# Scoring one attention unit ahead of the mix before it, and fetching value weights on GpSimd's queue

## The chip, the cores and the metric

One core of a Trainium2 chip runs the whole kernel in one launch. The metric is the device time of that launch in microseconds (us); the figure for a kernel is the median over its runs. The engines are called PE (TensorE, the matmuls), DVE (VectorE), ACT (ScalarE), POOL (GpSimd) and SP (SyncE, which here only issues transfers).

## The reference

The inputs are float32: 2048 tokens of width 512, 32 heads of 16 channels, and a feed-forward block with 1792 hidden channels. Each token attends to eight tokens: itself and those 2, 4, ... 14 positions before it.

```python
idx = pos[:, None] - (jnp.arange(8) * 2)[None, :]
logits = jnp.einsum("bhsd,bhswd->bhsw", q, k[:, :, idx]) * Dh ** -0.5
logits = jnp.where(idx >= 0, logits, -1e9)
a = jnp.einsum("bhsw,bhswd->bhsd", softmax(logits), v[:, :, idx]) @ wo
b = (gelu(x @ w_gate) * (x @ w_up)) @ w_down
g = sigmoid((x * gate_w).sum(-1, keepdims=True))
return g * a + (1 - g) * b
```

## The kernel before, in words

**Two parities.** Since the attention step is 2, even and odd tokens never meet. The kernel treats them as two parities, 0 and 1, of 1024 tokens each, and goes through keys and values of parity 0, its feed-forward block `ffn(0)`, then keys (`keys(1)`), values (`values(1)`) and `ffn(1)` of parity 1. At the end `out_first` and `finish` multiply the attention output of parity 0 and of parity 1 with `wo`. All products keep float32 accuracy by splitting each operand into a high and a low part and doing three matmuls.

**The feed-forward block** runs over 14 blocks of 128 hidden channels. For each, seven gate and up products of parts of the weights go to PSUM (L749), ACT copies them out with `copy` and `add` (L754, L760), DVE adds them (L761, L765), ACT takes the Gelu (L866) and the factor (L850), and DVE and ACT split the product into `hh` and `hl`. For each pair of blocks, `down` multiplies them with `w_down` (L798) into four accumulators `acc` and four banks `p` whose sums ACT saves and reloads (L792, L813).

**The attention runs on DVE beside that.** A parity has four units of 128 channels (8 heads), written (0,0) to (1,3). A unit is done in three steps:

- `scores` (L536, L539): four multiplies of the queries with eight shifted keys in tile `kq`, each followed by a sum over the head's 16 channels, into the tile `lg`; `lg` has two buffers, `kq` one.
- `softmax`: max (L550), subtract (L552), Exp on ACT (L554), sum (L555), reciprocal (L557), for parity 1 the gate (L559), multiply (L561). One tile `m` of one buffer holds max and sum.
- `mix`: loads the values into the tile `v` (one buffer) with two transfers (L520, L521), then four times a multiply (L575) and three adds (L579, L581, L583); after each two of these a transpose (L588) into `tb`, and four stores `os<-tb` on SP (L590).

`channels` reads a stored half unit back (`raw<-os`, L1008), splits it (L87 on ACT, L88 on DVE) and so gives `out_first` and `finish` their operands (matmuls at L1030). `load_o` splits `wo` (L231, L132 on ACT) and lets transfers on POOL's queue form the low parts (L232).

**What sets the order.** `attention()` is a generator; after each DVE step it yields an estimate of that step's time. The feed-forward code calls `pull(budget)` at fixed places, which emits as many attention steps as the budget pays for, at a lower priority. A scheduler then decides the order of the instructions on each engine from priorities, its own model of the times, and the buffers of the pools. After that, each engine works through its list strictly in that order. Before the change, `attention()` handles unit after unit: softmax of unit i, `load_kq` of unit i+1 if its keys are there, mix of unit i, scores of unit i+1.

**Value weights.** `values` of parity 1 needs 14 parts of weights of 258 KB each that were stored to device memory earlier; `fetch_v` (L207, L209) reads them back during `keys(1)` and the start of `values(1)`, into the tiles `c`, `g0` and `g1`.

Of the kernel before, what the change touches and what calls it, by code (L numbers as in the profile page):

```python
# [10 lines left out]
F32 = mybir.dt.float32  # L11
# [5 lines left out]
P = 128  # L17
# [3 lines left out]
NP = NT // 2  # L21
# [6 lines left out]
UC = 128  # L28
UH = UC // DH
# [2 lines left out]
BEHIND = 150  # L32
PACE = (1.05, 1.22)
LOAD = 4.0
BT = 4
MASKED = -1e9 * DH ** 0.5
LOWS = (4, 8, 10), (4, 6, 8, 10, 12)
# [8 lines left out]
def tile_gated_mix(ctx: ExitStack, tc: tile.TileContext, xt, wqkv, wff, wo, out):  # L46
    nc = tc.nc
    ctx.enter_context(nc.allow_non_contiguous_dma(reason="rows of 512 bytes"))
    pool = ctx.enter_context(tc.tile_pool(name="sb", bufs=1))
# [15 lines left out]
    def bank(tag):  # L65
        return psum.tile([P, 512], F32, name=tag, bufs=BUFS.get(tag, 1))
# [30 lines left out]
    for par in range(2):  # L97
# [4 lines left out]
        for u in range(NU):  # L102
            for half in range(2):
                OS[par, u, half] = dram.tile([4, 32, 4, BT * 32], F32, name=f"os{par}{u}{half}")

# [34 lines left out]
    VW, VR, VO, SLOT = 2 * WQ, {}, {}, []  # L140
# [17 lines left out]
    def load_v(*names):  # L158

        if not PLACES:  # L160
            t = pool.tile([P, 2 * NP - 1, UC], F32, name="v").rearrange("p a c -> p (a c)")
            u = pool.tile([P, 2, BT * UC], F32, name="tb").rearrange("p a c -> p (a c)")
            PLACES.extend([t[:, i * VW:(i + 1) * VW] for i in range(3)] + [u[:, :VW]])
# [35 lines left out]
    VS_W, keep_v = {}, []  # L199
# [6 lines left out]

    def fetch_v(n):  # L207
        for i in range(2):
            nc.sync.dma_start(VO[n][i].bitcast(F32), VS_W[n][i])  # L209

# [136 lines left out]
    def values(par, bg, step, ks=range(7)):  # L349
# [14 lines left out]
        def stage():  # L364
            return tl(next(stages))[:, :512]

        def copy(o, i):
            nc.scalar.activation(o, i, AF.Copy)

        def store(st, jj, hh):  # L370
            nc.sync.dma_start(rows(VS[par, hh][:, W:], jj), st.rearrange("p (c d) -> p c d", c=2))

        for k, (a, b) in enumerate((("a11", "b11"), ("a12", "b21"), ("s1", "t1"), ("s4", "b22"), ("s2", "t2"),
                                    ("s3", "t3"), ("a22", "t4"))):
            if k not in ks:
                continue
            for t in range(BT):
                if k == 0:
# [24 lines left out]
                elif k == 5:  # L403
                    copy(US[t][:, :CU], ps[:, :CU])
                    nc.vector.tensor_tensor(PS[t], PS[t], US[t], op=OP.add)
                    store(PS[t][:, CU:], t, 1)
                    store(PS[t][:, :CU], BT + t, 1)
                else:
                    if k == 1 or not par:
                        ST[t] = stage()  # L410
                    jj, st = (t, ST[t][:, :CU]) if k == 1 else (BT + t, ST[t][:, CU:])
                    copy(st, ps[:, :CU])
# [16 lines left out]
    def keys(prep, bg):  # L429
# [4 lines left out]
        for k, (a, b) in enumerate(KEYS[:5]):  # L434
# [3 lines left out]
            if k == 0:  # L438
                C.update((t, bank(f"acc{t}")) for t in range(BT))
                for t in range(BT):  # L440
# [62 lines left out]
    LG = {}  # L503

    def load_kq(par, u):
        hh, c = divmod(u, 2)
        kq = KQ.pop() if KQ else pool.tile([P, 3 * NP - 1, UC], F32, name="kq")
        k, q = kq[:, :2 * NP - 1], kq[:, 2 * NP - 1:]
        LG[par, u] = k, q
        if not (par or u):  # L510

            nc.gpsimd.memset(k[:1, :NP - 1], 0.0)
            for a, b in (1, P - 15), (P - 15, P):
                nc.sync.dma_start(k[a:b, :NP - 1], k[a - 1:b - 1, NP:])
            return
        load_slots(k, KS[par, hh][c], paced)
        paced(nc.sync.dma_start(q, QS[par, hh][c].rearrange("(p j) d -> p j d", j=NP)))

    def load_slots(t, src, hold=lambda x: x):
        hold(nc.sync.dma_start(t[:, :NP - 1], src[:S // 2].rearrange("(p j) d -> p j d", j=NP)[:, 1:]))  # L520
        hold(nc.sync.dma_start(t[:, NP - 1:], src[W:].rearrange("(p j) d -> p j d", j=NP)))  # L521

    def spans(t, jj):

        a = t[:, jj:jj + W, :]
        return bass.AP(a.tensor, a.offset, [a.ap[0], [UC, 2], [UC, W], [1, UC]])

    def two_of(lg, jj):
        return lg[:, :, jj:jj + 2].rearrange("p h j w -> p (j w) h")

    def scores(par, u):
        k, q = LG[par, u]
        lg = pool.tile([P, UH, NP, W], F32, name="lg", bufs=2)
        for jj in range(0, NP, 2):
            prod = pool.tile([P, 2, W, UC], F32, name="prod")
            paced(nc.vector.tensor_tensor(prod, spans(k, jj), q[:, jj:jj + 2, None, :].to_broadcast([P, 2, W, UC]),  # L536
                                          op=OP.mult))
            yield 2.3
            nc.vector.tensor_reduce(two_of(lg, jj), prod.rearrange("p j w (h d) -> p (j w) h d", d=DH), axis=AX.X,  # L539
                                    op=OP.add)  # L540
            yield 2.3
        first = lg[:1, :, :NP - 1, :W - 1]
        nc.vector.tensor_tensor(first, first, mask[:1, None, :NP - 1, :W - 1].to_broadcast([1, UH, NP - 1, W - 1]),
                                op=OP.min)
        LG[par, u] = lg

    def softmax(par, u):
        lg = LG[par, u]
        m = pool.tile([P, UH, NP], F32, name="m")
        nc.vector.tensor_reduce(m, lg, axis=AX.X, op=OP.max)  # L550
        yield 0.7
        nc.vector.tensor_tensor(lg, lg, m[:, :, :, None].to_broadcast([P, UH, NP, W]), op=OP.subtract)  # L552
        yield 0.7
        nc.scalar.activation(lg, lg, AF.Exp, scale=DH ** -0.5)  # L554
        nc.vector.tensor_reduce(m, lg, axis=AX.X, op=OP.add)  # L555
        yield 0.7
        nc.vector.reciprocal(m, m)  # L557
        if par:
            nc.vector.tensor_tensor(m, m, g[:, par, None, :].to_broadcast([P, UH, NP]), op=OP.mult)  # L559
        yield 0.4  # L560
        nc.vector.tensor_tensor(lg, lg, m[:, :, :, None].to_broadcast([P, UH, NP, W]), op=OP.mult)  # L561
        yield 0.7

    def mix(par, u, pause):
        lg = LG.pop((par, u))
        hh, c = divmod(u, 2)
        v = pool.tile([P, 2 * NP - 1, UC], F32, name="v")
        load_slots(v, VS[par, hh][c])
        yield pause
        tb = pool.tile([P, 2, BT * UC], F32, name="tb")  # L570
        for jj in range(0, NP, 2):
            if jj % BT == 0:
                o = pool.tile([P, 4, BT, 32], F32, name="o")
            prod = pool.tile([P, 2, W, UC], F32, name="prod")
            paced(nc.vector.tensor_tensor(prod.rearrange("p j w (h d) -> p (j w) h d", d=DH),  # L575
                                          spans(v, jj).rearrange("p j w (h d) -> p j w h d", d=DH),
                                          two_of(lg, jj)[:, :, :, None].to_broadcast([P, 2 * W, UH, DH]), op=OP.mult))
            yield 2.3
            nc.vector.tensor_tensor(prod[:, :, :4], prod[:, :, :4], prod[:, :, 4:], op=OP.add)  # L579
            yield 1.2  # L580
            nc.vector.tensor_tensor(prod[:, :, :2], prod[:, :, :2], prod[:, :, 2:4], op=OP.add)  # L581
            two = [prod[:, :, i].rearrange("p j (b c) -> p b j c", b=4) for i in range(2)]
            nc.vector.tensor_tensor(o[:, :, jj % BT:jj % BT + 2], *two, op=OP.add)  # L583
            yield 1.1

            if jj % BT == BT - 2:
                t = tb[:, jj // BT]
                nc.vector.transpose(t, o.rearrange("p b t c -> p (b t c)"))  # L588
                for a in range(4):
                    nc.sync.dma_start(OS[par, u, jj // BT][:, :, a].rearrange("b i c -> i b c"),  # L590
                                      t[32 * a:32 * a + 32].rearrange("p (b c) -> p b c", b=4))
                yield 0.7

    done = set()
# [13 lines left out]
    def need(*key):  # L608
        while key not in done:
            yield None  # L610

    def attention():
        units = [(0, u) for u in range(NU)] + [(1, u) for u in range(NU)]
        yield from need(0, 0)
        yield from scores(0, 0)
        yield from need(0, 1)
        scored, mixed = 1, False
        for i, un in enumerate(units):
            if scored == i:
                yield from need(un[0], un[1] // 2 * 2)  # L620
                load_kq(*un)
                yield LOAD
                yield from scores(*un)
                scored += 1
                mixed = False
            yield from need(un[0], 1)
            yield from softmax(*un)


            to = units[scored] if scored < len(units) else None  # L630
            ahead = i and to and (to[0], to[1] // 2 * 2) in done
            if ahead:
                load_kq(*to)
            yield from mix(*un, LOAD if mixed else 0.0)
            done.add((*un, "o"))
            mixed = not ahead
            if ahead:
                yield from scores(*to)
                scored += 1

    fill = attention()
    credit, FILL, AFTER = [0.0], [], []

# [447 lines left out]
    for kc in range(KC):  # L1091
        name, i = ("b11", "b21")[kc // 2], kc % 2
# [222 lines left out]
```

## Time and profile before

| what | value |
|---|---|
| median of 3 runs | 611.03 us (609.93 to 612.69) |
| profiled execution, own time | 608.94 us |
| its span | 607.2 us |
| mean granted TensorE clock | 0.991 |
| PE busy | 589.2 us, 97% of the span |
| DVE busy | 535.0 us, 88% |
| ACT busy | 426.6 us, 70% |
| POOL busy | 122.8 us, 20% |
| DMA | 142.76 MB, mean 235 GB/s |

The profile shows one execution. Its rows name a line of the kernel, the engine, the operation, and output and input tiles. A timeline row has the start, the busy time, and in brackets the idle time before it on that engine and who ended it. A waits row has the sum, the number and the longest of the waits of one kind. "PEld" is the loading of weights into TensorE, which overlaps the matmuls. "SPq" or "POOLq" is the queue in which an engine issues transfers; the time shown is that of the issue, and "us to landing" is from there until the data is in place.

### The profile page before, as it was taken

What the parts mean: (1) busy time and instruction counts of PE and PEld (TensorE: products, weight loads), DVE (VectorE), ACT (ScalarE), POOL (GpSimd) and SP (SyncE); (2) the same over time, 40 slices, a digit from 0 to 9 for tenths busy, and PEclk for the clock granted to TensorE, in tenths of its full rate; (3) what the DMA queues carried; (4) which work ended last, traced back from release to release, by engine and by line L of the source; (5) the groups of instructions that cost most, each with busy time, mean ns of one, the idle gap of its engine ahead of it and who ended that gap; (6) DMA issues with size and microseconds to landing.
All of it is one profiled execution on the core that took longest, in us unless ns stands there. A gap on an engine that the chain in (4) does not pass through costs nothing.

```text
span 607.2 us, 8273 instructions
## 1 busy us (share of the span) xinstructions
PE 589.2 (97%) x2743; PEld 490.5 (81%) x2743; DVE 535.0 (88%) x623; ACT 426.6 (70%) x755; POOL 122.8 (20%) x143
## 2 busy tenths in 40 slices
PE   9999999999999999999999999999999999989983
PEld 7889888888888888888888878888878888868872
DVE  6989988999899987999978998999699979979790
ACT  6778677677888778868658646777787687945611
POOL 0230840121012120112003831121212121303100
PEclk9999999999999999999999999999999999999996
DMA  8789999898978988999898999688978998887424
GB/s 308 228 234 287 314 302 257 244 259 218 271 211 251 244 243 189 278 306 322 241 340 249 253 256 290 165 237 212 252 196 221 238 247 224 208 212 138 53 62 146
DMA packets 89320, 142.76 MB, mean 235 GB/s; under 512 B 8639, under 2 KB 49983, under 8 KB 89278
## 3 DMA queue, kind: packets, MB, share of 16 engines
q1 hardware_dynamic: 67470, 106.91, 54.1%
q0 software_dynamic: 21520, 34.94, 32.2%
q8 instruction: 21, 0.34, 0.2%
q10 hardware_dynamic: 288, 0.39, 0.2%
q14 instruction: 21, 0.17, 0.1%
HBM read 69.83 MB, written 46.49 MB: 192 GB/s over the span
## 4 chain that ended last, share of the span: by engine, by line
PE 85%; DMA 7%; ACT 3%; issue 2%; POOL 2%; SPq 0%; DVE 0%; POOLq 0%; ACTq 0%
PE p L749 39%; PE acc L798 12%; PE p L798 12%; PE acc L475 9%; PE p L1030 5%; PE p L361 3%; DMA qs<-rt 2%; PE acc L361 2%; PE p L475 2%; PE acc L1030 2%; DMA S<-raw 1%; DMA raw<-os 1%; POOL qs L483 1%; DMA g<-ws 1%; DMA g<-vwt 1%
## 5 line engine op out<-in xcount | busy, mean ns | idle before, releaser
L749 PE MATMUL p<-S,g 128*128 128x512 f32 x672 | 167.7, 389 | 0.0
L749 PEld LDWEIGHTS p<-S,g 128*128 128x128 f32 x672 | 125.8, 188 | 25.7
L749 PE MATMUL p<-A,g 128*128 128x512 f32 x504 | 126.1, 390 | 0.2 <-ACT c L760 0.2
L749 PEld LDWEIGHTS p<-A,g 128*128 128x128 f32 x504 | 94.3, 188 | 20.3 <-ACT c L760 0.7
L575 DVE TENSOR_TENSOR prod<-v,lg 128x2048 f32<-128x2048 f32 x32 | 72.9, 2278 | 0.6
L539 DVE TENSOR_REDUCE lg<-prod 128x128 f32<-128x2048 f32 x32 | 73.0, 2281 | 0.2
L536 DVE TENSOR_TENSOR prod<-kq 128x2048 f32<-128x2048 f32 x32 | 72.9, 2277 | 0.1
L798 PE MATMUL p<-d,hh 128*128 128x512 f32 x224 | 68.2, 390 | 0.2 <-ACT p L792 0.2
L708 POOL DMA_DIRECT2D g<-raw x26 | 22.5, 866 | 211.3 <-ACT g L705 101.8
L798 PE MATMUL acc<-d,hh 128*128 128x512 f32 x224 | 59.4, 389 | 0.0
L760 ACT ACTIVATE c<-p 128x512 f32<-128x512 f32 x56 | 33.5, 597 | 35.1 <-PE p L749 35.0
L798 PEld LDWEIGHTS p<-d,hh 128*128 128x128 f32 x224 | 42.0, 188 | 9.3 <-ACT p L792 0.7
L798 PEld LDWEIGHTS acc<-d,hh 128*128 128x128 f32 x224 | 42.1, 188 | 8.7
L761 DVE TENSOR_TENSOR c<-c,s 128x512 f32<-128x512 f32 x56 | 37.9, 684 | 5.6 <-ACT c L760 5.4
L798 PE MATMUL p<-d,hl 128*128 128x512 f32 x112 | 42.0, 390 | 0.0
L765 DVE TENSOR_TENSOR c<-c 128x512 f32<-128x512 f32 x56 | 38.3, 684 | 2.1 <-ACT c L866 2.0
L579 DVE TENSOR_TENSOR prod<-prod 128x1024 f32<-128x1024 f32 x32 | 39.0, 1220 | 0.1
L754 ACT ACTIVATE s<-p 128x512 f32<-128x512 f32 x56 | 33.1, 593 | 7.0 <-PE p L749 6.8
L475 PE MATMUL acc<-d,S 128*128 128x512 f32 x144 | 35.2, 391 | 0.1
L798 PE MATMUL acc<-d,hl 128*128 128x512 f32 x112 | 35.1, 389 | 0.0
L813 ACT ACTIVATE rt<-p 128x512 f32<-128x512 f32 x48 | 28.0, 595 | 9.6 <-PE p L798 9.3
L740 POOL DMA_DIRECT2D d<-r x23 | 20.1, 873 | 68.9 <-ACT d L739 54.4
(219 smaller groups left out, 1064.4 us busy)
## 6 DMA issues: line engine op xcount, KB each, us to landing
g<-raw POOLq DMA_DIRECT2D x26, 512.0 KB, 6.9
ws<-g SPq DMA_DIRECT2D x14, 768.0 KB, 6.0
g<-ws SPq DMA_DIRECT2D x14, 768.0 KB, 7.7
r<-wff SPq DMA_DIRECT2D x28, 256.0 KB, 4.4
raw<-wff SPq DMA_DIRECT2D x14, 512.0 KB, 4.7
d<-r POOLq DMA_DIRECT2D x23, 256.0 KB, 7.2
ws<-raw SPq DMA_DIRECT2D x14, 384.0 KB, 5.3
raw<-ws SPq DMA_DIRECT2D x14, 384.0 KB, 4.4
```

Source lines behind the costliest of these rows:

```text
L475: LAST[:] = [nc.tensor.matmul(ps, x[:, ts], w, start=(start and kc == i == 0), stop=(kc == 1 and i == 2), skip_group_check=True)]
L536: paced(nc.vector.tensor_tensor(prod, spans(k, jj), q[:, jj:jj + 2, None, :].to_broadcast([P, 2, W, UC]), op=OP.mult))
L539: nc.vector.tensor_reduce(two_of(lg, jj), prod.rearrange("p j w (h d) -> p (j w) h d", d=DH), axis=AX.X, op=OP.add)
L575: paced(nc.vector.tensor_tensor(prod.rearrange("p j w (h d) -> p (j w) h d", d=DH), spans(v, jj).rearrange("p j w (h d) -> p j w h d", d=D ...
L579: nc.vector.tensor_tensor(prod[:, :, :4], prod[:, :, :4], prod[:, :, 4:], op=OP.add)
L749: LAST[:] = [nc.tensor.matmul(ps, w_, a_, start=(start and kc == 0 and n == 0), stop=(kc == 1 and n == 2), skip_group_check=True)]
L754: nc.scalar.activation(s, ps, AF.Copy)
L760: nc.scalar.activation(c, ps, AF.Copy)
L761: nc.vector.tensor_tensor(c, c, s, op=OP.add)
L765: nc.vector.tensor_tensor(ge, ge, up, op=OP.mult)
L798: LAST[:] = [nc.tensor.matmul(pp, a[:, ts], w, start=(i == 0 and n == 0 and gr == 0), stop=(i == 1 and n == 2), skip_group_check=True)]
L1030: LAST[:] = [nc.tensor.matmul(pa, a, b, start=(first and n == 0), stop=(last and n == 2), skip_group_check=True)]
```

## The change

The softmax is cut in two: `exps` (max, subtract, Exp) and `shares` (sum, reciprocal, gate, multiply). The loading of `v` is taken out of `mix` into `load_values`. From unit 1 on (`PIPE = 1`, counted over all eight units), if the keys of the next unit are there, `attention()` emits: values of unit i, scores of unit i+1, keys of unit i+2, max, subtract and Exp of unit i+1, then the mix of unit i, then sum, reciprocal and multiply of unit i+1. Unit (0,0) keeps the old order. `fetch_v` issues on GpSimd's queue instead of SyncE's. No arithmetic changes. Lines further down move by about 32 numbers: L749 becomes L781, L798 L830, L1030 L1062, L575 L585, L554 L557, L1008 L1040.

```diff
@@ -32,6 +32,9 @@
 BEHIND = 150
 PACE = (1.05, 1.22)
 LOAD = 4.0
+
+
+PIPE = 1
 BT = 4
 MASKED = -1e9 * DH ** 0.5
 LOWS = (4, 8, 10), (4, 6, 8, 10, 12)
@@ -206,7 +209,7 @@
 
     def fetch_v(n):
         for i in range(2):
-            nc.sync.dma_start(VO[n][i].bitcast(F32), VS_W[n][i])
+            nc.gpsimd.dma_start(VO[n][i].bitcast(F32), VS_W[n][i])
 
 
 
@@ -544,7 +547,7 @@
                                 op=OP.min)
         LG[par, u] = lg
 
-    def softmax(par, u):
+    def exps(par, u):
         lg = LG[par, u]
         m = pool.tile([P, UH, NP], F32, name="m")
         nc.vector.tensor_reduce(m, lg, axis=AX.X, op=OP.max)
@@ -552,6 +555,10 @@
         nc.vector.tensor_tensor(lg, lg, m[:, :, :, None].to_broadcast([P, UH, NP, W]), op=OP.subtract)
         yield 0.7
         nc.scalar.activation(lg, lg, AF.Exp, scale=DH ** -0.5)
+
+    def shares(par, u):
+        lg = LG[par, u]
+        m = pool.tile([P, UH, NP], F32, name="m")
         nc.vector.tensor_reduce(m, lg, axis=AX.X, op=OP.add)
         yield 0.7
         nc.vector.reciprocal(m, m)
@@ -561,12 +568,15 @@
         nc.vector.tensor_tensor(lg, lg, m[:, :, :, None].to_broadcast([P, UH, NP, W]), op=OP.mult)
         yield 0.7
 
-    def mix(par, u, pause):
-        lg = LG.pop((par, u))
+    VT = {}
+
+    def load_values(par, u):
         hh, c = divmod(u, 2)
-        v = pool.tile([P, 2 * NP - 1, UC], F32, name="v")
+        VT[par, u] = v = pool.tile([P, 2 * NP - 1, UC], F32, name="v")
         load_slots(v, VS[par, hh][c])
-        yield pause
+
+    def mix(par, u):
+        lg, v = LG.pop((par, u)), VT.pop((par, u))
         tb = pool.tile([P, 2, BT * UC], F32, name="tb")
         for jj in range(0, NP, 2):
             if jj % BT == 0:
@@ -611,32 +621,54 @@
 
     def attention():
         units = [(0, u) for u in range(NU)] + [(1, u) for u in range(NU)]
+        scored, ready, shared = [0], [], []
+
+        def keyed(i):
+            return i < len(units) and (units[i][0], units[i][1] // 2 * 2) in done
+
+        def logits(i):
+            if units[i] not in LG:
+                load_kq(*units[i])
+                yield LOAD
+            yield from scores(*units[i])
+            scored.append(i)
+
         yield from need(0, 0)
         yield from scores(0, 0)
         yield from need(0, 1)
-        scored, mixed = 1, False
+        mixed = False
         for i, un in enumerate(units):
-            if scored == i:
+            if i not in scored:
                 yield from need(un[0], un[1] // 2 * 2)
-                load_kq(*un)
+                yield from logits(i)
+                mixed = False
+            if i not in ready:
+                if i >= PIPE and keyed(i + 1):
+                    load_kq(*units[i + 1])
+                yield from exps(*un)
+            yield from need(un[0], 1)
+            if i not in shared:
+                yield from shares(*un)
+            pipe, ahead = i >= PIPE and keyed(i + 1), i and keyed(i + 1)
+            if not pipe and ahead:
+                load_kq(*units[i + 1])
+            load_values(*un)
+            if pipe:
+                yield from logits(i + 1)
+                if keyed(i + 2):
+                    load_kq(*units[i + 2])
+                yield from exps(*units[i + 1])
+                ready.append(i + 1)
+            elif mixed:
                 yield LOAD
-                yield from scores(*un)
-                scored += 1
-                mixed = False
-            yield from need(un[0], 1)
-            yield from softmax(*un)
-
-
-            to = units[scored] if scored < len(units) else None
-            ahead = i and to and (to[0], to[1] // 2 * 2) in done
-            if ahead:
-                load_kq(*to)
-            yield from mix(*un, LOAD if mixed else 0.0)
+            yield from mix(*un)
             done.add((*un, "o"))
             mixed = not ahead
-            if ahead:
-                yield from scores(*to)
-                scored += 1
+            if pipe:
+                yield from shares(*units[i + 1])
+                shared.append(i + 1)
+            elif ahead:
+                yield from logits(i + 1)
 
     fill = attention()
     credit, FILL, AFTER = [0.0], [], []
```

Where the instructions stand now is shown at three places near the end, all around unit (1,3), the last one.

**VectorE, from the last scores of unit (1,3).** `kq`, `lg_5041` (before) and `lg_4856` (after) belong to unit (1,3), `v_4853` and `lg_4337` to unit (1,2). Before:

```order
L539 TENSOR_REDUCE lg_5041<-prod_5192 128x16x8
L543 TENSOR_TENSOR lg_5041<-lg_5041,mask_102 1x8x7x7
L550 TENSOR_REDUCE m_5251<-lg_5041 128x64
L552 TENSOR_TENSOR lg_5041<-lg_5041,m_5251 128x512
L555 TENSOR_REDUCE m_5251<-lg_5041 128x64
L557 RECIPROCAL m_5251<-m_5251 128x64
L559 TENSOR_TENSOR m_5251<-m_5251,g_136 128x64
L88 TENSOR_TENSOR hl_5601<-raw_5526,hh_5600 128x4x4x32
L561 TENSOR_TENSOR lg_5041<-lg_5041,m_5251 128x512
L575 TENSOR_TENSOR prod_5299<-v_5294,lg_5041 128x2048
```

After:

```order
L585 TENSOR_TENSOR prod_5066<-v_4853,lg_4337 128x2048
L553 TENSOR_REDUCE m_5054<-lg_4856 128x64
L589 TENSOR_TENSOR prod_5066<-prod_5066 128x2x512
L555 TENSOR_TENSOR lg_4856<-lg_4856,m_5054 128x512
L591 TENSOR_TENSOR prod_5066<-prod_5066 128x2x256
L793 TENSOR_TENSOR c_5129<-c_5129,s_5099 128x512
L593 TENSOR_TENSOR o_5065<-prod_5066 128x4x64
L797 TENSOR_TENSOR c_5119<-c_5119,c_5129 128x512
L585 TENSOR_TENSOR prod_5121<-v_4853,lg_4337 128x2048
L562 TENSOR_REDUCE m_5297<-lg_4856 128x64
L793 TENSOR_TENSOR c_5148<-c_5148,s_5075 128x512
L589 TENSOR_TENSOR prod_5121<-prod_5121 128x2x512
```

Before, sum stands directly behind subtract, with Exp on another engine between them, and the mix follows. Now the mix of unit (1,2) stands there: its first multiply ahead of the max, its adds between max, subtract and sum.

**ScalarE, the Exp of unit (1,3).** Before, it stands late, among the copies of `out_first` (L1047) and the scalings of the accumulators (L802):

```order
L1047 ACTIVATE s_5500<-p_5487,g_136 128x512
L792 ACTIVATE p_5576<-rt_3962 128x512
L554 ACT_TABLE_LOAD
L554 ACTIVATE lg_5041<-lg_5041 128x512
L1047 ACTIVATE r_5516<-p_5503,g_136 128x512
L802 ACTIVATE acc0_3735<-acc0_3735,gc_137 128x512
```

After, it stands in the last feed-forward blocks:

```order
L742 ACTIVATE g1_5101<-raw_4917 128x1024
L845 ACTIVATE rt_3825<-p_5133 128x512
L557 ACT_TABLE_LOAD
L557 ACTIVATE lg_4856<-lg_4856 128x512
L792 ACTIVATE c_5148<-p_5042 128x512
```

and the next Gelu needs its table back, in a stretch that leads to the splits of `wo` (the tiles `g1_5182`, `S_5234`):

```order
L135 ACTIVATE g1_5182<-raw_5039 128x512
L898 ACT_TABLE_LOAD
L898 ACTIVATE c_5218<-p_5042 128x512
L786 ACTIVATE s_5207<-p_5200 128x512
L234 ACTIVATE g1_5182<-raw_5039 128x512
L135 ACTIVATE g1_5182<-raw_5039 128x512
L824 ACTIVATE p_5283<-rt_3953 128x512
L786 ACTIVATE s_5232<-p_5170 128x512
L234 ACTIVATE S_5234<-raw_5039 128x512
L135 ACTIVATE S_5234<-raw_5039 128x512
L234 ACTIVATE S_5248<-raw_5039 128x512
```

The same stretch before has no table loads in it:

```order
L132 ACTIVATE g1_5188<-raw_5055 128x512
L866 ACTIVATE c_5218<-p_5058 128x512
L792 ACTIVATE p_5285<-rt_3962 128x512
L754 ACTIVATE s_5207<-p_5200 128x512
L231 ACTIVATE g1_5188<-raw_5055 128x512
L132 ACTIVATE g1_5188<-raw_5055 128x512
L773 ACTIVATE hl_5222<-c_5218 128x512
L775 ACTIVATE hh_5221<-c_5218 128x512
L754 ACTIVATE s_5232<-p_5176 128x512
L231 ACTIVATE S_5234<-raw_5055 128x512
L132 ACTIVATE S_5234<-raw_5055 128x512
```

What moved is one table load and the Exp, and one further table load is new in this stretch. Over the whole kernel ACT has 20 table loads now and had 17.

**SyncE, the values of unit (1,3).** Before, `v_5294` is loaded ahead of the reads that serve `out_first` and `finish`:

```order
L1008 DMA raw_5262<-os030_119 128x512
L520 DMA v_5294<-vs11_125 128x896
L521 DMA v_5294<-vs11_125 128x1024
L590 DMA os121_132<-tb_4785 32x4x128 x4
L1008 DMA raw_5432<-os001_114 128x512
L1008 DMA raw_5432<-os011_116 128x512
L1008 DMA raw_5432<-os021_118 128x512
L1008 DMA raw_5432<-os031_120 128x512
L1008 DMA raw_5526<-os100_127 128x512
L1008 DMA raw_5526<-os101_128 128x512
L1008 DMA raw_5526<-os110_129 128x512
L1008 DMA raw_5526<-os111_130 128x512
```

After:

```order
L1040 DMA raw_5534<-os100_127 128x512
L1040 DMA raw_5534<-os101_128 128x512
L1040 DMA raw_5534<-os110_129 128x512
L1040 DMA raw_5534<-os111_130 128x512
L523 DMA v_5329<-vs11_125 128x896
L524 DMA v_5329<-vs11_125 128x1024
L1040 DMA raw_5636<-os120_131 128x512
L600 DMA os121_132<-tb_5064 32x4x128 x4
L1040 DMA raw_5636<-os121_132 128x512
L600 DMA os130_133<-tb_5332 32x4x128 x4
L1040 DMA raw_5636<-os130_133 128x512
```

The load of `v` (now `v_5329`) moved behind the reads into `raw_5435` and `raw_5534`.

On GpSimd's queue the fetches L212 stand between and behind the eight stores of parity 0's feed-forward result (L841); the first weight sum of `ffn(1)` (L740) stands behind the last of them.

## The prediction

> **What bounds the kernel now.** I read the page's busy times first, then the waits of PE, then the chain that ended last, then the timelines of the places that these named.
>
> ```profile
> PE 589.2 (97%) x2743; PEld 490.5 (81%) x2743; DVE 535.0 (88%) x623; ACT 426.6 (70%) x755; POOL 122.8 (20%) x143
> ```
>
> PE is busy for 589.2 us of a span of 607.2, so at most 18 us are to be had without fewer matmuls. The change removes none, so it can only act on the idle time of PE. The waits of PE (sum, number, longest) show where that is:
>
> ```profile
> PE p L1030 <- ACT hh L87: 8.1, 1, 8.1
> PE p L1030 <- DMA S<-raw: 2.1, 2, 1.9
> PE acc L361 <- DMA g<-vwt: 1.2, 1, 1.2
> ...
> PE p L1030 <- ACT rt L813: 0.9, 1, 0.9
> PE p L798 <- ACT p L792: 0.2, 1, 0.2
> PE p L749 <- ACT c L760: 0.2, 1, 0.2
> ```
>
> One wait has more than half of it: 8.1 us ahead of the last matmuls of `finish`. The chain around that wait, and then two stretches of the windows view (behind the length, PE busy and its count; the granted clock stands behind the engines):
>
> ```profile
> 578.54 3.40 PE p L1030 x15
> ...
> 592.96 1.80 DMA os<-tb
> 594.90 2.61 DMA raw<-os
> 598.22 4.99 PE p L1030 x12
> ```
>
> ```profile
> 590.00:598.20 8.20, 0.10 (x1) 0.00 (x0) 1.57 (x4) 1.17 (x3) 0.00 (x0) 0.64 0.56 192
> 598.20:603.20 5.00, 4.97 (x12) 3.61 (x12) 1.38 (x2) 1.19 (x2) 0.00 (x0) 0.57 0.23 88
> ```
>
> From 590.1 to 598.2 PE has nothing left but the 12 matmuls of the last half unit, and its operand comes by a store, a read back and a split. What releases that chain is DVE, the end of the mix of unit (1,3):
>
> ```profile
> 551.98 0.68 DVE L769 TENSOR_TENSOR hl<-c,hh 128x512 fp32r<-128x512 f32 x1
> ...
> 568.11 2.29 DVE L575 TENSOR_TENSOR prod<-v,lg 128x2048 f32<-128x2048 f32 x1
> ...
> 590.29 0.70 DVE L588 STREAM_TRANSPOSE tb<-o 128x512 f32<-128x512 f32 x1
> ```
>
> So attention ends too late by 8.1 us, and nowhere else does it hold PE up visibly. The 12 matmuls also run slowly after the idle time: 4.99 us, 0.42 each, at a granted clock of 0.57, where 15 took 3.40, 0.227 each, shortly before.
>
> **Part 1: the wait for Exp, eight times.**
>
> ```profile
> L555 DVE TENSOR_REDUCE m<-lg 128x64 f32<-128x512 f32 x8 | 5.5, 686 | 25.9 <-ACT lg L554 25.9
> ```
>
> DVE stands idle for 25.9 us in eight units, 3.2 each, behind Exp. With another unit's mix between subtract and sum these go for the six units from (0,2) on, about 19 us of DVE; (0,0) and (0,1) keep theirs. While `ffn` runs this is worth nothing by itself, since PE does not wait for DVE there; `pull` paces the attention by the feed-forward code. It counts only as a lead at the end.
>
> **Part 2: the lead at the end.** The last step of the feed-forward block on DVE is the split at 551.98. Before, DVE finishes unit (1,3) at 590.99, 39.0 us later. After, only the mix of (1,3) and the last transpose of (1,2) stand behind that split. Their durations:
>
> ```profile
> L539 DVE TENSOR_REDUCE lg<-prod 128x128 f32<-128x2048 f32 x32 | 73.0, 2281 | 0.2
> L575 DVE TENSOR_TENSOR prod<-v,lg 128x2048 f32<-128x2048 f32 x32 | 72.9, 2278 | 0.6
> L579 DVE TENSOR_TENSOR prod<-prod 128x1024 f32<-128x1024 f32 x32 | 39.0, 1220 | 0.1
> L581 DVE TENSOR_TENSOR prod<-prod 128x512 f32<-128x512 f32 x32 | 22.0, 688 | 0.4
> L583 DVE TENSOR_TENSOR o<-prod 128x256 f32<-128x256 f32 x32 | 13.5, 422 | 0.6
> L588 DVE STREAM_TRANSPOSE tb<-o 128x512 f32<-128x512 f32 x16 | 11.3, 709 | 0.4
> ```
>
> Four times 2.28 + 1.22 + 0.69 + 0.42 is 18.4; three transposes are 2.1; seven more splits of the size of that at 551.98 are 4.8; with that split itself it is 26.0 us. If the feed-forward block is where it was, the last transpose ends at 578; if it is 2 us late (part 4), at 580. From the end at 590.99 to PE at 598.22 the chain took 7.2 us, so its operand is there at 587.2. PE comes to the last 12 matmuls at 590.1 + 2. The 8.1 us go whole, with 5 us to spare, and so do 4.99 − 12 × 0.227 = 2.3 us of slow matmuls. Gain 10.4. The next late thing is PE itself.
>
> **Part 3: what eats the lead.** `v` has one buffer. Before, the mix of (1,3) starts at 568.11 without a wait for it.
>
> ```profile
> 539.25 8.04 SPq L1008 DMA_DIRECT2D raw<-os  x10
> ```
>
> ```profile
> v<-vs SPq DMA_DIRECT2D x8, 512.0 KB, 6.5
> ```
>
> After, the load stands behind eight of the reads that began at 539.25. These reads wait for a `raw` buffer that `wo` holds. Eight tenths of 8.04 is 6.4, and the reads start about 3 late (part 4), so the issue is at 549 and the landing 6.5 later, near 555. DVE would want `v` at about 553 to 555. I take 1 us of wait, with 0 to 6 as bounds; the 5 us of slack cover most of this. The other units have a whole set of scores, four multiplies of the size of the mix's and four sums (L539), 8 × 2.28 = 18.2 us, ahead of their mix, to cover a 6.5 us load.
>
> Eight stores of results then close up behind each other where they were spread over 590 to 604; I add 0.5 us, an estimate between 0 and the 2 us that one read of the same size takes (2.61 above).
>
> **Part 4: Exp and its tables on ACT.** Before, the Exp of (1,3) stands at 563, where ACT idles. Now it stands ahead of the splits of `wo`:
>
> ```profile
> 518.50:530.00 11.50, 11.50 (x52) 9.55 (x51) 11.47 (x15) 11.42 (x23) 4.09 (x5) 1.00 0.84 219
> ```
>
> ```profile
> 529.91 0.63 ACT L231 ACTIVATE S<-raw 128x512 fp32r<-128x512 f32 x1
> ...
> 537.99 0.96 PE L1030 MATMUL p<-S,A 128*128 128x512 f32 x3 [1.85 <-DMA S<-raw]
> ```
>
> ACT (its busy time stands fourth) is busy for 11.42 of the 11.5 us up to the split at 529.91, POOL's transfer for it lands at 538, and PE already waits 1.85 for it. The additions, from the Exp of (0,2):
>
> ```profile
> 228.62 1.28 ACT L554 ACT_TABLE_LOAD   x1
> 229.91 0.63 ACT L554 ACTIVATE lg<-lg 128x512 f32<-128x512 f32 x1
> 230.56 1.28 ACT L850 ACT_TABLE_LOAD   x1
> 231.86 0.60 ACT L850 ACTIVATE c<-p 128x512 f32<-128x512 f32 x1
> ```
>
> From 228.62 to 231.86 it is 3.2 us for Exp with its two loads. So `S<-raw` lands 3.2 later, and PE waits up to 3.2 longer. Of this I take 2, since PE waits 0.9 again at 546 for ACT and 2.1 in sum here, and a later arrival shares these gaps; bounds 0 and 5 (ACT might also wait for DVE's subtract, which now stands behind a mix multiply of 2.28). The Trainium skill ("ScalarE: Activation LUTs", What ACT_TABLE_LOAD costs) speaks against the change more strongly: a switch of tables is to cost a load of about 1283 ns and a drain of about 1380. Two switches would then put 2.8 us more in this stretch, and the sum below would end at 607.9. The rows show the next ACTIVATE 1.29 and 1.30 us after the start of the load: the load agrees, a drain behind it does not show, and the measurement decides.
>
> In the middle, five more Exps move to other places. Each sits in ACT's list behind a subtract that DVE does between mix instructions, so ACT may wait up to a 2.28 multiply, and the copies that empty PSUM queue behind it. Before, seven such Exps with their loads cost PE no more than the 0.2 + 0.2 us at the end of its waits. ACT idles 35.0 us for PE in 34 places:
>
> ```profile
> ACT c L760 <- PE p L749: 35.0, 34, 3.1
> ```
>
> That is 1 us of slack each time, which absorbs a short delay but not a whole multiply. The third unit's keys also have less cover: its scores follow the max of (0,1) at once. I take 2 us in sum on PE, with 0 and 11.5 (five times 2.3) as bounds, nearer the low one, by the two waits of 0.2.
>
> **Part 5: the fetches.** SP gets rid of 14 issues and these waits (sum, number, longest):
>
> ```profile
> SPq L209 <- DMA out<-c: 8.3, 4, 3.5
> ```
>
> ```profile
> 323.45 0.88 POOL L708 DMA_DIRECT2D g<-raw  x1 [43.62 <-ACT hl L368]
> ```
>
> POOL idles 43.62 us ahead of 323.45, so it has room for 14 issues at under 0.9 each; but a fetch into a `c` buffer now holds up the `out` stores behind it. PE waited 1.2 us for one fetched part, the 1.2 in the list of waits above: I take 0, between a gain of 1.2 and a loss of 2.
>
> **The sum.** 608.94 − 8.1 − 2.3 + 0.5 + 2 + 2 = 603.0 for an execution like the profiled one. Its time is 2.09 below the median of the runs shown (611.03), so the forecast is **605.1 us**, 1.0% faster. All penalties at zero give 600.6, with the fetch wait gone 599.4.
>
> **Rivals.**
>
> *ACT stalls PE in every unit (slower).* The place is the Exp of each of the units from (0,2) on: it waits in order for a subtract that DVE reaches only after a mix multiply, while all copies out of PSUM are behind it. If DVE lags the plan by one multiply, five Exps cost 2.3 us each, 11.5, and the stretch before `wo` its 5: the forecast without stalls in the middle is 603.1, so 603.1 + 3 + 11.5 = 617.6. Slower by over 0.5% begins at 614.1; with the 5 that is (614.1 − 606.1) / 5 = 1.6 us for each Exp. For it: ACT is full for 11.5 us before the split of `wo`. Against it: Exps cost PE almost nothing before.
>
> *The gain is handed back at the end (about the same).* `v` of (1,3) lands 6 us late and the reads behind `wo` slide by 2 more; the last transpose ends at 588, the operand is there at 595.2, PE waits 3.1 and runs its last matmuls slowly again: 605.1 + 3.1 + 2.3 = 610.5. For it: the one buffer of `v` and eight reads ahead of it. Against it: 5 us of slack.
>
> *The whole gain, or more.* PE hides all additions: 600.6. For it: PE's waits were tiny throughout. Against it: `S<-raw` already ends a wait of 1.85.
>
> **How the numbers follow.** About 0.5% of the median, 3 us, is what a measurement of this kernel can tell from no change. Forecast as summed, between 602 and 607.5: 0.37. Whole gain: 0.15. Handed back, or middle stalls of 5 to 7 us, 608 to 614: 0.25. Slower by stalls: 0.23. The first two make faster 0.52. The range from 600.5 to 614.5 leaves out the worse part of the slower case and the end of the best one. If it is faster at all, the likeliest range is 601 to 607.5.
>
> **What would show it.** Right: among PE's waits, the 8.1 for `hh` is gone or under 2, the granted clock in the last 10 us is near 1, the 25.9 on the sum's row is under 8, and the last transpose ends 8 to 12 us earlier. Part 4 is right if the wait for `S<-raw` is 4 to 5 us. Part 3 shows as a DVE wait for `v` of a few us in the tail. The forecast is wrong if PE's waits for copies by ACT (`c`, `rt`, `p`, `hh`) add up to over 10 us in the middle of the kernel, or if a wait for the last `hh` remains.

## The result

The changed kernel takes 607.97 us in the median of 14 executions (605.78 to 610.80), the kernel before 612.02 (609.93 to 613.92). The ratio is 0.9936, with a 95% interval of 0.9918 to 0.9953: 0.6% faster, where 1.0% was forecast. The profiled execution of the changed kernel took 609.9 us (span 607.7), above its median, and that of the kernel before 608.94, below all of its timed ones, so the two spans are almost equal and the profiles are compared by stage, not by their ends.

First the waits of PE in the changed kernel (sum, number, longest):

```profile
PE p L781 <- DMA g<-raw: 2.9, 1, 2.9
PE acc L830 <- DMA hl<-c: 2.2, 1, 2.2
PE p L1062 <- ACT c L792: 2.2, 1, 2.2
PE p L781 <- ACT c L792: 1.8, 2, 1.4
PE p L781 <- ACT p L867: 1.7, 1, 1.7
PE p L830 <- ACT p L824: 1.0, 1, 1.0
```

The 8.1 us for the last `hh` and the waits for `S<-raw` and for a fetched part `g<-vwt` are gone. In their place stand other waits, 11.8 us in these six rows, 8.3 of them ahead of 380 us. The end, in the chain and in DVE's timeline:

```profile
592.91 2.72 PE acc L1062 x12
601.07 2.73 PE p L1062 x12
```

```profile
559.44 0.69 DVE L801 TENSOR_TENSOR hl<-c,hh 128x512 fp32r<-128x512 f32 x1
...
560.68 2.25 DVE L585 TENSOR_TENSOR prod<-v,lg 128x2048 f32<-128x2048 f32 x1
...
586.39 0.70 DVE L598 STREAM_TRANSPOSE tb<-o 128x512 f32<-128x512 f32 x1
```

The last 12 matmuls take 2.73 us instead of 4.99, without idle time ahead of them. From the last split of the feed-forward block to the last transpose DVE needs 27.6 us instead of 39.0. But that split itself is at 559.44 instead of 551.98. So what was won at the end had been lost before it. The windows view shows the largest loss (PE busy and its matmuls stand behind the length). Before:

```profile
350.00:360.00 10.00, 9.77 (x44) 7.77 (x43) 8.60 (x8) 5.67 (x9) 5.23 (x5) 1.00 1.21 249
360.00:370.00 10.00, 10.00 (x46) 8.29 (x45) 10.00 (x9) 4.49 (x7) 0.00 (x0) 1.00 1.12 292
```

After:

```profile
350.00:360.00 10.00, 9.04 (x39) 6.69 (x37) 7.91 (x11) 8.84 (x14) 5.78 (x5) 1.00 1.16 319
360.00:370.00 10.00, 5.90 (x20) 4.49 (x21) 8.12 (x13) 6.60 (x12) 0.89 (x1) 0.90 0.95 164
```

PE does 59 matmuls in these 20 us instead of 90, where `ffn(1)` begins. 31 matmuls at 0.227 us are 7 us. Only 5.1 us of that are idle time; after it the matmuls run slower, and the granted clock of the second stretch is 0.90. Two smaller losses are the 2.2 us for `hl<-c` at 236.6 and 1.0 us for `p<-rt` at 271.

### The profile page after: what moved, and what is told of

Same layout as the page of the kernel before. It is cut to its first block, busy times and chain, and to the rows that moved or that the text cites. A ratio compares the mean times of both kernels' runs of the same rounds, so it can differ in the third digit from the quotient of the medians.

```text
span 607.7 us, 8282 instructions
## 1 busy us (share of the span) xinstructions
PE 590.8 (97%) x2743; PEld 491.3 (81%) x2743; DVE 533.5 (88%) x623; ACT 430.0 (71%) x758; POOL 130.1 (21%) x157
## 4 chain that ended last, share of the span: by engine, by line
PE 79%; DMA 6%; ACT 6%; DVE 5%; issue 3%; POOL 1%; POOLq 0%; DVEq 0%; ACTq 0%
PE p L781 33%; PE p L830 10%; PE acc L830 10%; PE acc L478 9%; PE p L1062 6%; PE p L364 3%; PE acc L364 3%; DMA g<-raw 2%; DMA qs<-rt 2%; PE p L478 2%; PE acc L1062 2%; DMA hl<-c 2%; DVE lg L542 1%; DVE prod L539 1%; ACT L557 1%
## 5 line engine op out<-in xcount | busy, mean ns | idle before, releaser
L781 PE MATMUL p<-S,g 128*128 128x512 f32 x672 | 169.8, 391 | 2.2 <-ACT p L867 1.7
L781 PEld LDWEIGHTS p<-S,g 128*128 128x128 f32 x672 | 126.0, 189 | 29.4 <-ACT p L867 2.2
L781 PE MATMUL p<-A,g 128*128 128x512 f32 x504 | 128.4, 392 | 4.3 <-DMA g<-raw 2.9
L781 PEld LDWEIGHTS p<-A,g 128*128 128x128 f32 x504 | 94.4, 188 | 25.2 <-DMA g<-raw 3.6
L585 DVE TENSOR_TENSOR prod<-v,lg 128x2048 f32<-128x2048 f32 x32 | 72.8, 2274 | 1.5 <-PE acc L830 1.1
L830 PE MATMUL p<-d,hh 128*128 128x512 f32 x224 | 68.3, 390 | 1.0 <-ACT p L824 1.0
L830 PE MATMUL acc<-d,hh 128*128 128x512 f32 x224 | 59.4, 390 | 0.0
L740 POOL DMA_DIRECT2D g<-raw x26 | 23.6, 907 | 165.2 <-ACT g L737 129.0
L830 PEld LDWEIGHTS p<-d,hh 128*128 128x128 f32 x224 | 42.0, 188 | 10.2 <-ACT p L824 1.5
L830 PEld LDWEIGHTS acc<-d,hh 128*128 128x128 f32 x224 | 42.2, 188 | 8.9
L830 PE MATMUL p<-d,hl 128*128 128x512 f32 x112 | 42.4, 389 | 0.0
L830 PE MATMUL acc<-d,hl 128*128 128x512 f32 x112 | 34.1, 390 | 2.2 <-DMA hl<-c 2.2
L845 ACT ACTIVATE rt<-p 128x512 f32<-128x512 f32 x48 | 28.0, 595 | 11.5 <-PE p L830 11.0
```

The source lines that it names most:

```text
L781: LAST[:] = [nc.tensor.matmul(ps, w_, a_, start=(start and kc == 0 and n == 0), stop=(kc == 1 and n == 2), skip_group_check=True)]
L830: LAST[:] = [nc.tensor.matmul(pp, a[:, ts], w, start=(i == 0 and n == 0 and gr == 0), stop=(i == 1 and n == 2), skip_group_check=True)]
```

## The experiments

In the kernels with pipelining the condition is written once as `piped(i)`, with the instructions of the changed kernel in the same order, and its first part is varied; their lines lie up to three further down. Each ratio is to the kernel before, run on the same chip (611.5 to 612.0 us in the median on each).

### The change in two halves

**The changed kernel again**, for a second profile.

> The changed kernel once more, with the same instructions in the same order on every engine, for a second profile. Both theories: 608 us (before 612). Theory A (the gain is the wait and the slow matmuls at the end; the loss is a hole in PE around 355 to 375 us, where ffn(1) begins): the hole of about 8 us is there again, and the 2.2 us wait for hl at 237 too. If the hole is an accident of one execution, PE loses under 3 us there.

Measured: 606.22 us, ratio 0.9912 (0.9883 to 0.9941). Its profiled execution took 603.85. The losses stand at the same places, but are smaller: 72 matmuls from 350 to 370, where the first profile has 59 and the kernel before 90, and these waits:

```profile
PE p L784 <- ACT p L870: 1.7, 1, 1.7
PE acc L833 <- DMA hl<-c: 1.1, 1, 1.1
...
PE p L784 <- DMA g<-raw: 0.6, 1, 0.6
```

The wait for `p`, a copy by ACT, is as long as before; the two for transfers are much shorter. So the hole comes with this order of the kernel, 4 to 7 us deep in two executions; that may be a part of the spread of 5 us among its executions.

**Only the fetches**, no pipelining:

```diff
-PIPE = 1
+PIPE = 99
```

> Only the fetches move to GpSimd's queue; no unit is scored ahead of a mix (PIPE = 99). Theory A: the fetches are worth about the 1.2 us that PE waited for a fetched part, so 610.5 to 612, and the 8 us wait for the last hh stays. Theory B (the fetches bring the gain, and pipelining brings as much as it costs): 608, with PE ahead by 3 us or more at 330.

Measured: **601.69 us**, ratio 0.9847 (0.9826 to 0.9868). Neither theory had this: the fetches alone are worth 10 us, and pipelining on top of them loses 4 to 6. The wait for the last `hh` is shorter, and none for `S<-raw` is left:

```profile
PE p L1065 <- ACT hh L90: 4.8, 1, 4.8
```

**Only the pipelining**, the fetches on SyncE:

```diff
-            nc.gpsimd.dma_start(VO[n][i].bitcast(F32), VS_W[n][i])
+            nc.sync.dma_start(VO[n][i].bitcast(F32), VS_W[n][i])
```

> Only the pipelining; the fetches stay on SyncE's queue. Theory A: 608 to 610, the last wait is gone, and the hole around 355 to 375 is as large, since the scores of unit (1,0) stand there ahead of the mix of (0,3). Theory B: 612. If the hole comes from GpSimd's queue being late after the fetches, it is gone here, and the time is 603 to 605.

Measured: 608.30 us, ratio 0.9946 (0.9924 to 0.9968). The hole at 360 to 370 is there (PE waits 3.9 us for `g<-raw`), so it does not come from GpSimd's queue. With pipelining, the fetches are worth next to nothing.

**No pipelining across the parities:**

```diff
-            return i >= PIPE and keyed(i + 1)
+            return i >= PIPE and i != 3 and keyed(i + 1)
```

> As the changed kernel, but the mix of (0,3) comes ahead of the scores of (1,0): no pipelining from one parity to the next. Theory A: the hole where ffn(1) begins shrinks from 8 us to under 2 and the end stays as it is: 601 to 603 us. If the hole has another cause (GpSimd's queue, a crowd of transfers), it stays: 607 to 609.

Measured: 611.86 us, ratio 0.9997 (0.9977 to 1.0018). Neither figure held. The hole stays (4.8 us of wait for `g<-raw`), so my theory that it comes from the scores of (1,0) standing ahead of the mix of (0,3) fell. The kernel is even 4 to 6 us slower than with this pair, so the pair across the parities gains here.

### Queue or order: why 14 fetches are worth 10 us

The scheduler orders by its own model of the times, so moving a fetch can change the order of other instructions. By its lists, moving the two of `t2` makes it arrange PE, ACT and DVE otherwise from `values(1)` on; moved alone, those of `b22` change PE's list only, and each of the others changes none of the three. These moves were not run one by one. This allows a test of the queue without the order, and of the order with as little of the queue as possible. In the profiles, PE, ACT and DVE go through their operations in the same sequence in the kernel before and in the first of these two, and in the kernel with all fetches moved and in the second.

**Ten of 14 fetches moved, the order of the kernel before:**

```diff
-            nc.sync.dma_start(VO[n][i].bitcast(F32), VS_W[n][i])
+            (nc.gpsimd if n in ('b11','b21','t1','t3','t4') else nc.sync).dma_start(VO[n][i].bitcast(F32), VS_W[n][i])
```

> The kernel before with 10 of its 14 fetches (all but b22 and t2) on GpSimd's queue; PE, ACT and DVE keep the order of the kernel before, instruction by instruction. Theory Q (the queue itself brings the 10 us of the fetches alone): 603 to 605. Theory O (moving t2 makes the scheduler choose another order, and the order brings it): 610 to 611.5, with the wait of 8 us for the last hh.

Measured: 611.80 us, ratio 0.9994 (0.9976 to 1.0012), the wait for the last `hh` 8.5 us.

**Four moved, the order of the kernel with all moved:**

```diff
-            nc.sync.dma_start(VO[n][i].bitcast(F32), VS_W[n][i])
+            (nc.gpsimd if n in ('b22','t2') else nc.sync).dma_start(VO[n][i].bitcast(F32), VS_W[n][i])
```

> The kernel before with only b22 and t2 (4 of 14 fetches) on GpSimd's queue; PE, ACT and DVE have the order of the kernel with all fetches moved and no pipelining. Theory Q: 608 to 610. Theory O: 601 to 603, attention ends about 7 us earlier than in the kernel before.

Measured: **601.59 us**, ratio 0.9827 (0.9804 to 0.9851). With ten fetches the queue is worth nothing that can be measured, and the order with four has all 10 us. Those four on GpSimd's queue in the old order were not run; PE had waited 1.2 us for a fetched part and does not here, which is all that their queue is seen to give directly. What the order does is seen in the waits and on DVE, where the wait for Exp had been 25.9 us and the one for the last `hh` 8.1:

```profile
DVE m L555 <- ACT lg L554: 18.9, 8, 4.0
...
PE p L1030 <- ACT hh L87: 4.7, 1, 4.7
```

```profile
547.61 1.29 DVE L769 TENSOR_TENSOR hl<-c,hh 128x512 fp32r<-128x512 f32 x2
...
583.24 0.71 DVE L588 STREAM_TRANSPOSE tb<-o 128x512 f32<-128x512 f32 x1
```

Exp is waited for 7 us less, without any pipelining; the last splits of the feed-forward block end at 548.9 instead of 552.7; PE no longer waits for `S<-raw`; attention ends 7 us earlier. Which of these differences in the order brings which part of the 10 us was not separated.

### Which pairs cost and which gain

All of these have all fetches moved, so 601.7 is the measure.

**The last pair alone**, `PIPE = 6`.

> All fetches moved, and only the last pair is pipelined: the scores of (1,3) ahead of the mix of (1,2) (PIPE = 6). Theory P (every pair in the middle costs PE time in ACT's list, and only the last pair gains): the last wait of 4.8 us and 1.8 us of slow matmuls go, the Exp among the splits of wo costs 1 to 4: 597 to 600. Theory D (each change of the order is a draw, whatever the pair): 601 to 607.

Measured: 602.52 us, ratio 0.9843 (0.9819 to 0.9868): no gain, in the range of theory D. Three rows tell why:

```profile
561.57 2.29 DVE L585 TENSOR_TENSOR prod<-v,lg 128x2048 f32<-128x2048 f32 x1 [4.53 <-DMA v<-vs]
```

```profile
536.05 2.45 PE L1065 MATMUL p<-g,A 128*128 128x512 f32 x6 [3.31 <-ACT c L795]
...
592.86 0.73 PE L1065 MATMUL p<-S,hh 128*128 128x512 f32 x2 [3.20 <-ACT hh L90]
```

DVE waits 4.5 us for values that can no longer be fetched ahead, PE waits 3.3 for a copy by ACT that stands, at 535.41, behind the Exp among the splits of `wo` and its two table loads (530.12 to 533.36), and 3.2 of the last wait are left. The prediction's parts 3 and 4 are both seen here, each at its own price.

**The pairs of parity 0 alone**, `i in (1, 2)`.

> All fetches moved, and only the pairs (0,1)-(0,2) and (0,2)-(0,3) are pipelined. Theory P: the losses of the changed kernel at 237, 275 and 355 to 375 are all there (about 8 to 10 us) and the end is as with the fetches alone: 608 to 612. If those losses come from the later pairs, none of them shows and it is 601 to 603.

Measured: 620.51 us, ratio 1.0146 (1.0120 to 1.0171). These two pairs cost 19 us, more than either theory had. The middle has its losses (5.2 us for `g<-raw` alone), and the end is worse as well: 8.1 us of wait for the last `hh`, and 2.4 for `S<-raw`, as in the kernel before.

**The first pair alone**, `i == 1`.

> All fetches moved, only the pair (0,1)-(0,2) is pipelined. The losses at 237 and 275 (together 3 us) should be there, since they stand at the Exp and the copies of (0,2). If the hole at 355 to 375 needs the Exp of (0,3) to be early, it is absent: 603 to 606. If any pair in parity 0 makes it: 611 to 620.

Measured: 616.39 us, ratio 1.0083 (1.0057 to 1.0110). The time is in the second range, but not for its reason: there is no hole at 355 to 375, but another at 240. DVE first, then ACT and PE:

```profile
236.39 2.29 DVE L585 TENSOR_TENSOR prod<-v,lg 128x2048 f32<-128x2048 f32 x1 [6.72 <-DMA v<-vs]
...
239.86 0.68 DVE L796 TENSOR_TENSOR c<-c,s 128x512 f32<-128x512 f32 x1
...
241.07 0.68 DVE L800 TENSOR_TENSOR c<-c 128x512 f32<-128x512 f32 x1
```

```profile
241.79 0.63 ACT L803 ACTIVATE hh<-c 128x512 fp32r<-128x512 f32 x1 [6.13 <-DVE c L800]
```

```profile
242.47 3.78 PE L833 MATMUL acc<-d,hh 128*128 128x512 f32 x8 [4.79 <-ACT hh L803]
```

The mix of (0,2) waits 6.7 us for its values, the adds of the feed-forward block stand behind it on DVE, ACT waits for them and PE for ACT. A value load that is late costs PE time in the middle of `ffn`, too: from 230 to 250 PE does 56 matmuls, where the kernel with the fetches alone does 88. And the end is worse: the last wait for `hh` is 9.3 us instead of 4.8. Why a change in the first parity lengthens that wait was not tried; the order of the whole end differs again.

**The second pair alone**, `i == 2`.

> All fetches moved, only the pair (0,2)-(0,3) is pipelined. The loss at 237 is absent, since the order up to there is that of the kernel before. If the hole at 355 to 375 needs both pairs: 601 to 604. If this pair alone makes it: 608 to 618.

Measured: 619.10 us, ratio 1.0125 (1.0103 to 1.0146). This pair alone makes the hole at 355 to 375, at a price just above the range, and the last wait for `hh` is 9.2 us here too. The third load of weight sums for `ffn(1)`, with the fetches alone (SP, then POOL):

```profile
330.65 0.45 SPq L762 DMA_DIRECT2D raw<-ws  x1
...
343.93 0.89 POOL L743 DMA_DIRECT2D g<-raw  x1 [0.59 <-PE p L784]
```

and with the second pair pipelined (SP, SP, POOL, PE):

```profile
337.35 0.92 SPq L374 DMA_DIRECT2D vs<-hl  x1
...
339.20 0.77 SPq L762 DMA_DIRECT2D raw<-ws  x1
```

```profile
352.93 0.89 POOL L743 DMA_DIRECT2D g<-raw  x1 [1.10 <-PE p L784]
```

```profile
366.16 4.21 PE L784 MATMUL p<-A,g 128*128 128x512 f32 x9 [6.43 <-DMA g<-raw]
```

In both kernels the load stands behind the last of the 16 stores of the values of parity 1 (`vs`) on SP; here it is 8.6 us later, the transfer that forms the low part is issued 9.0 us later, and PE waits 6.4 us for it. What came ahead of the last twelve of those stores on SP is the value load of (0,3) and the last stores of (0,2). With the fetches alone they had been issued long before `ffn(1)`:

```profile
264.52 0.42 SPq L523 DMA_DIRECT2D v<-vs  x1
...
266.03 2.31 SPq L600 DMA_DIRECT2D os<-tb  x4
```

With the second pair pipelined, the mix of (0,2) moved behind the scores of (0,3), and they stand here:

```profile
319.42 0.38 SPq L523 DMA_DIRECT2D v<-vs  x1
...
320.57 2.14 SPq L600 DMA_DIRECT2D os<-tb  x4
```

SP's waits ahead of the `vs` stores (L374) fit this. With the fetches alone the longest are for operands that DVE and ACT make (3.3 and 2.4 us); with the second pair the longest are for other transfers to land:

```profile
SPq L374 <- DMA g<-ws: 2.8, 1, 2.8
...
SPq L374 <- DMA v<-vs: 2.2, 2, 1.1
...
SPq L374 <- DMA os<-tb: 1.7, 1, 1.7
```

That the crowd makes the stores late is argued from these rows; it was not tried by itself. The mix of (0,3) also starts late, at 327.57 after 4.5 us of waiting for its values, and at 321.95 with the fetches alone.

**The table loads ahead of the hole.** Since the Exp of (0,3) comes early, the small Exp of the gate (L427) needs its own load of the table, and the Gelu behind it another. With a Copy both loads vanish, and nothing else changes its place (the result then lacks the Exp of parity 1's gate):

```diff
-        nc.scalar.activation(en, z[:, par], AF.Exp, scale=-1.0)
+        nc.scalar.activation(en, z[:, par], AF.Copy if par else AF.Exp, scale=-1.0)
```

> The changed kernel with the one small Exp of parity 1's gate (L427) done as a Copy, so its output leaves the gate's Exp out. All engines keep the order of the changed kernel; only two table loads of ACT are gone, which stand there because the Exp of (0,3) came long before. Theory E (these loads start the hole at 355 to 375 by making ACT late): the hole shrinks from 4 to 8 us to under 2, time 600 to 603. Theory F (the hole is made by the order of the loads and copies around the start of ffn(1)): the loads' own 2.6 us at most, 604 to 608.

Measured: 607.59 us, ratio 0.9933 (0.9910 to 0.9957), as the changed kernel itself. The hole is as deep as in the second profile of the changed kernel (71 matmuls from 350 to 370). Theory E fell; even the 2.6 us of the loads themselves do not show.

**The two pairs inside `ffn(1)`**, `i in (4, 5)`.

> All fetches moved, only the pairs (1,0)-(1,1) and (1,1)-(1,2), both inside ffn(1), are pipelined. Theory P in its mild form (pairs inside ffn(1) cost nothing, and give back some of DVE's wait for Exp): 600 to 602, and the last wait of 4.8 us shrinks by 2 to 4. Theory D (any change of the order is a draw): 603 to 612.

Measured: **598.29 us** (597.44 to 605.31; four of six executions between 597.4 and 598.7, two at 604.0 and 605.3), ratio 0.9816 (0.9774 to 0.9859), below the figures of both theories. The only waits of PE left, and the end:

```profile
PE p L784 <- ACT p L870: 1.9, 1, 1.9
PE p L76 <- DVE warm L73: 1.0, 1, 1.0
```

```profile
577.51 0.71 DVE L598 STREAM_TRANSPOSE tb<-o 128x512 f32<-128x512 f32 x1
```

```profile
580.62 2.72 PE acc L1065 x12
588.78 2.73 PE p L1065 x12
```

Attention ends 13 us earlier than in the kernel before, and nothing is waited for at the end. It has the lowest median of all and beats both kernels, but its interval overlaps that of the fetches alone, so that these two pairs gain is not shown. (A second buffer for `v` was not run.)

## Why the prediction was right, and where it was not

The sign held. The time, 607.97, lies 2.9 above the forecast and 0.5 above the range of 601 to 607.5 that was called likeliest for a faster kernel, inside the whole range. The end gave what was stated, 10.4 us. The middle cost about 10 us in the first profile and 6 in the second, where 2 were taken. Two smaller parts made up for some of that: the splits of `wo` cost 0.6 instead of 2, and the 1.2 us of waiting for a fetched part went, where 0 was taken. That both fell on the good side is luck. What happened is thus a whole gain at the end and stalls of 6 to 10 us in the middle, a mixture that the prediction weighed only at 5 to 7 us of stalls, and there with 608 to 614 us.

**What bounds, and part 2 (the lead): right.** PE was bound, and the last wait went whole with its slow matmuls: 8.1 + 2.3 us, as stated. DVE's path from the last split to the last transpose was 27.6 us, where 26.0 was worked out. The last operand was ready at 594.5, when its split on DVE ended, and PE came to its last 12 matmuls at 601.07: 6.5 us to spare, where 5 were worked out. One sign failed: the last transpose ended 3.9 us earlier than before and not 8 to 12, because the feed-forward block came 7.5 us later, and PE with it.

**Part 1: right.** The row of the sum:

```profile
L562 DVE TENSOR_REDUCE m<-lg 128x64 f32<-128x512 f32 x8 | 5.5, 682 | 3.5 <-ACT lg L557 3.4
```

The idle time ahead of it fell from 25.9 to 3.5 us, under the 8 that were named.

**Part 3: the mechanism was right, and it has more places.** In the changed kernel DVE did not wait for the values of (1,3) at all (560.68 has no wait), though its load was issued at 553.2 and not at 549, since the work ahead of it was late as well; with the last pair alone it waited 4.5 us, inside the bounds of 0 to 6. The other units did not wait for values in the changed kernel either, as the 18.2 us of scores were to ensure. The price falls on the unit with which a run of pipelined pairs ends: its load comes after the mix before it, and no scores stand behind it. With the first pair alone the load of (0,2) was issued at 222.6 and wanted at 229.7, and DVE waited 6.7; with the second pair (0,3) waited 4.5, with the two pairs inside `ffn(1)` unit (1,2) waited 5.2, and there PE did not notice.

**Part 4, the splits of `wo`: a smaller price, at another place.** The sign named, a wait of 4 to 5 us for `S<-raw`, did not come; that wait is gone. PE waits 1.4 us (532.74) for a copy by ACT directly behind the Exp and 2.2 (547.45) for one behind the splits, where before it waited 2.1 for `S<-raw` and 0.9 for ACT: 0.6 more in sum, where 2 were taken. Alone, in the last pair, the wait for ACT is 3.3. A table load costs its own 1.28 us: the next ACTIVATE begins 1.29 after its start, at 531.57 and 539.14. The drain of about 1380 ns that the Trainium skill ("ScalarE: Activation LUTs", What ACT_TABLE_LOAD costs) adds to a switch does not show here either.

```profile
530.28 1.28 ACT L557 ACT_TABLE_LOAD   x1
531.57 0.63 ACT L557 ACTIVATE lg<-lg 128x512 f32<-128x512 f32 x1
...
537.85 1.28 ACT L898 ACT_TABLE_LOAD   x1
539.14 0.60 ACT L898 ACTIVATE c<-p 128x512 f32<-128x512 f32 x1
```

**Part 4, the middle: the step that was priced is there, and another was left out.** "I take 2 us in sum on PE" was for copies that queue behind the Exps on ACT. Two such waits are seen, the longer one behind the Exp of (1,0):

```profile
358.74 1.28 ACT L557 ACT_TABLE_LOAD   x1
360.04 0.63 ACT L557 ACTIVATE lg<-lg 128x512 f32<-128x512 f32 x1
360.57 0.58 ACT L867 ACTIVATE p<-p 128x512 f32<-128x512 f32 x1
```

```profile
361.21 1.67 PE L781 MATMUL p<-S,g 128*128 128x512 f32 x6 [1.73 <-ACT p L867]
```

The other is the 1.0 us at 271, for a copy directly behind the Exp of (0,3) at 269.83. Together they are 2.8 us, in the second profile as well. But ACT did not stand waiting for DVE's subtract, as the prediction feared: no Exp has idle time ahead of it, and the copies are late by the load and the Exp themselves.

What the sum had no term for is transfers that land late in the new order: 2.2 us for `hl<-c` and 2.9 for `g<-raw` (1.1 and 0.6 in the second profile), with slower matmuls behind them. For `g<-raw` it is 3.9 to 6.4 us in four other kernels with the second pair. Its load is issued on SP at 338 to 342 us in all six of these profiles, and at 330.65 with the fetches alone. What makes `hl<-c` late stays open. The loss of the middle is inside the bounds (0 to 11.5), but these had been worked out from Exps alone. The rival that gave every Exp 2.3 us was wrong in its mechanism; that parity 0's pairs alone make the kernel 1.5% slower, near the size of that rival, is a coincidence.

**Part 5: right for the wrong kernel.** The queue of ten fetches is worth 0, as taken. What I had not weighed is that moving a transfer changes what the scheduler believes about times, and so the order of the compute engines: 10 us without pipelining, nothing that the two measurements of the changed kernel tell clearly from 0 with it (0.9936 and 0.9912 against 0.9946).

## What to carry to other kernels

Where a scheduler sets the order, an edit has two effects, the one that it names and the new order; compare the orders of the engines before pricing the edit, and look for a variant that has the new order without the edit, and one that has the edit without the order. Software pipelining moves the transfers of a step along with it: here the pairs inside one stage did no harm (598.3 us, against 601.7 without), and two pairs that end ahead of the next stage cost 19 us alone, at least in part through loads and stores that moved into that stage's queue. With one buffer, the last unit of a pipelined run loses its prefetch (waits of 4.5 to 6.7 us where one pair stood alone).

## What was not expected of the hardware

The queue of ten fetches made no difference (0.9994, 0.9976 to 1.0012) although SP had waited 8.3 us in the 14. One order of instructions gave five executions that agree within 0.2% (601.07 to 601.98) and another 14 that spread over 0.8% (605.78 to 610.80); the two profiles of the latter differ in how long PE waits for the same transfer, 0.6 and 2.9 us.
